# A new order of all steps, and single steps on another engine, in a gated linear attention with a mixing layer behind it

## The chip, the cores and the metric

The kernel runs on one core of a Trainium2 chip, in one launch. The metric is the device time of that core in microseconds (us). The kernel before took 360.42 us as the median of three runs (359.86 to 361.05). The core has five engines that work side by side, each on its own instructions in the order in which the program holds them: TensorE (PE in the profile; its weight loads are PEld), VectorE (DVE), ScalarE (ACT), GpSimd (POOL) and SyncE (SP), which here only issues the transfers.

## The reference

The inputs are q, k, v and gate logits of shape (4, 8, 768, 48), four weights and nothing else. First a gated linear attention runs over the 768 tokens, then its output goes through a mixing layer:

```python
f = 1.0 / (1.0 + np.exp(-f_logit))
for t in range(S):
    state = f[:, :, t, :, None] * state + np.einsum('bhd,bhe->bhde', k[:, :, t], v[:, :, t])
    y[:, :, t] = np.einsum('bhd,bhde->bhe', q[:, :, t], state)
...
theta = x @ w_theta
zr, zi = x * np.cos(theta), x * np.sin(theta)
y = np.einsum('ts,bsd->btd', w_tok_r, zr) + np.einsum('ts,bsd->btd', w_tok_i, zi)
u = x + y
return u + np.maximum(u @ w_ch, 0.0)
```

Here x is the attention's output with the 8 heads side by side (4, 768, 384). The weights come as float64, so that the kernel reads them as pairs of 32-bit words and decodes them to float32 itself. If some gate's product underflows, a second, slow program in the same kernel computes everything anew; it does not run on these inputs.

## The kernel before

The work is cut into 24 chunks of 128 tokens, six per batch. What is done for a chunk, and later for a group of three chunks (384 output tokens), is cut into named steps, each a small function. The table `ORDER` (line 53) lists 1169 step names; the loop at line 570 calls each step's function in that order, with a counter per name, so that the third `sc` is the scores of chunk 2. Since all five engines are scheduled by hand, the order of a step's instructions on its engine is its place in the table. A letter behind a slash says on which engine a step runs that could run on several: `/D` DVE, `/A` ACT, `/P` POOL; without one it is the usual engine of its function. Semaphores are set from the data: an instruction waits for what it reads and for the buffer that it writes, and for nothing else.

The steps that the prediction speaks of:

- `lf lq lk lv lw` load gates, q, k, v and a piece of a weight (SP).
- `gc go gs ge` turn the gate logits into running products: a clamp (line 237), two activations, a scan on DVE (247) and two activations (254, 255). `gp` copies the last column (POOL, 258).
- `gq` and `gk` multiply q (262) and k (267) by these products.
- `ke` transposes the keys (PE, 309), `kt` copies them out of PSUM; `sc` is the scores (298), `ma` their mask (304); `up` the state's update (323), `sa` and `st` add it (331, 335), `sm` fades the state (339); `qs` and `ou` are the output (354, 362), `xc` copies it, `xt` turns it (372), `xs` keeps it.
- `d1 d2 d3` decode a weight (183 and 193, 194 on DVE, 188 on ACT); `d4` and `d5` split it into a rounded part and a rest (218), since batches 1 to 3 use three products of rounded parts where batch 0 multiplies float32 as it is.
- `xh xl` split x (394), `th` is x @ w_theta (403), `tn se ab tr` reduce the angle and take sine and cosine, `ro` rotates x (436), `zh zl` split the result (443).
- `f0 f1 f2` are the token-mixing products (459), 48 of each; `v` adds them to x (463), `uh ul` split u (470), `c` is the channel product (477), `cv` the last addition (491), `so` the store (495).

What is on PE is therefore the same 4320 matmuls in any order. Tiles lie in pools with a fixed number of buffers: three each for f, q and k, one for the gates' products p, six for the rotated x and the weights' raw words, four banks of PSUM for the products.

Of the kernel before, what the change touches and what calls it, by code (L numbers as in the profile page):

```python
# [17 lines left out]
B, H, S, D = 4, 8, 768, 48  # L18
DM = H * D
P = 128  # L20
# [30 lines left out]


ORDER = (
# [36 lines left out]
)  # L90


# [608 lines left out]
```

## Time and profile before

| | before |
|---|---|
| median of three runs | 360.42 us |
| the profiled execution | 358.93 us |
| its span, from the first to the last instruction | 357.2 us |
| PE busy | 323.4 us (91%) |
| PEld busy | 284.8 us (80%) |
| DVE busy | 273.1 us (76%) |
| ACT busy | 186.6 us (52%) |
| POOL busy | 142.8 us (40%) |
| bytes moved | 45.55 MB |
| mean granted clock of TensorE | 0.980 of its 2.4 GHz |

The profile shows one execution. Busy time is the time in which an engine executes at least one instruction; the mean beside a group is that of one instruction from its start to its end, and instructions of one engine overlap a little, so the sum of a group's lengths is more than its busy time. An engine that waits for a semaphore is idle, but an instruction that has begun and is held up inside the engine counts as busy and shows as a longer one.

### The profile page before, as it was taken

The page shows a single profiled execution, that of the slowest core. Times are in us where ns is not written, and L with a number is a line of the kernel's source. Part 1 is how long each engine was busy: PE and PEld are TensorE (multiplying, and loading weights), DVE is VectorE, ACT ScalarE, POOL GpSimd, SP SyncE. Part 2 cuts the span into 40 slices and gives each one's busy share as a digit, 9 for nine tenths or more (in the row PEclk, how much of TensorE's full clock was granted, in tenths as well). Part 3 has the DMA queues.
Part 4 walks back from the last instruction along what each step waited for, and adds up shares of the span by engine and source line. Part 5 has one row for each costly group of instructions (what it writes and reads, how often), then busy time and mean ns, then how long its engine had stood idle before and what let it go on. Part 6 is the DMA issues. An engine that isn't in the chain of part 4 may idle for free.

```text
span 357.2 us, 10034 instructions
## 1 busy us (share of the span) xinstructions
PE 323.4 (91%) x4320; PEld 284.8 (80%) x4320; DVE 273.1 (76%) x402; ACT 186.6 (52%) x302; POOL 142.8 (40%) x122
## 2 busy tenths in 40 slices
PE   0689998799997699989999999999999999999992
PEld 0577675657754597978999999999999989999991
DVE  3999999999999989995889588996582766720331
ACT  5778988665856474846387252893224525200000
POOL 4426408660707705996588206604020512111000
PEclk9999999899999699999999999999999999999997
DMA  7888996158563225424040243503030200000112
GB/s 252 299 278 294 349 344 225 52 199 268 194 229 120 80 63 176 148 83 171 1 165 29 68 135 127 179 2 134 0 122 2 97 3 2 22 2 22 42 43 80
DMA packets 21651, 45.55 MB, mean 128 GB/s; under 512 B 2400, under 2 KB 5472, under 8 KB 21600
## 3 DMA queue, kind: packets, MB, share of 16 engines
q1 hardware_dynamic: 21600, 44.84, 37.0%
q8 instruction: 36, 0.59, 0.7%
q14 instruction: 15, 0.12, 0.1%
HBM read 40.11 MB, written 4.72 MB: 126 GB/s over the span
## 4 chain that ended last, share of the span: by engine, by line
PE 42%; DVE 5%; ACT 2%; DMA 1%; issue 1%; DVEq 0%; ACTq 0%
PE pm L459 23%; PE pch L477 8%; PE pth L403 4%; PE py L362 2%; DVE f L247 1%; PE sk L298 1%; PE pxt L372 1%; PE py L354 1%; PE sk L323 1%; PE psk L309 1%; DVE xl L394 1%; DVE k L267 1%; DMA out_dram<-ut 1%; DVE uhl L144 1%; DVE ut L491 0%
## 5 line engine op out<-in xcount | busy, mean ns | idle before, releaser
L459 PE MATMUL pm<-wp,z 128*128 128x384 f32 x648 | 119.2, 337 | 0.8 <-DVE ut L144 0.4
L459 PEld LDWEIGHTS pm<-wp,z 128*128 128x128 f32 x648 | 112.2, 188 | 2.0 <-DVE ut L144 0.8
L459 PE MATMUL pm<-value,z 128*128 128x384 f32 x144 | 49.9, 493 | 0.7 <-DVE value L194 0.7
L262 POOL TENSOR_TENSOR q<-q,p 128x512 f32<-128x512 f32 x20 | 31.1, 1553 | 39.0 <-ACT p L254 11.8
L459 PEld LDWEIGHTS pm<-value,z 128*128 128x128 f32 x144 | 27.1, 195 | 17.2 <-DVE value L194 1.4
L477 PE MATMUL pch<-uhl,wch 128*128 128x384 f32 x216 | 40.4, 339 | 0.0
L470 POOL TENSOR_TENSOR uhl<-ut,uhl 128x384 fp32r<-128x384 f32 x16 | 18.8, 1178 | 47.4 <-ACT uhl L144 35.0
L477 PEld LDWEIGHTS pch<-uhl,wch 128*128 128x128 f32 x216 | 37.4, 188 | 0.3
L247 DVE TENSOR_TENSOR_SCAN f<-carry,f 128x512 f32<-128x512 f32 x24 | 31.6, 1319 | 2.2 <-ACT f L243 2.2
L443 POOL TENSOR_TENSOR z<-w,z 128x768 fp32r<-128x768 f32 x12 | 23.6, 1970 | 21.8 <-ACT z L144 11.4
L309 PE MATMUL psk<-ident,k 128*128 128x128 f32 x96 | 16.9, 304 | 16.8 <-DVE k L267 16.5
L267 DVE SCALAR_TENSOR_TENSOR k<-f,k 128x512 f32<-128x512 f32 x24 | 27.6, 1150 | 2.8 <-ACT f L255 2.7
L491 DVE SCALAR_TENSOR_TENSOR ut<-pch,ut 128x384 f32<-128x384 f32 x24 | 13.0, 550 | 21.0 <-PE pch L477 20.9
L309 PEld LDWEIGHTS psk<-ident,k 128*128 128x128 f32 x96 | 12.0, 153 | 21.0 <-POOL q L262 9.3
L144 ACT CAST uhl<-ut 128x384 fp32r<-128x384 f32 x14 | 7.0, 508 | 41.1 <-PE pch L477 33.9
L436 DVE TENSOR_TENSOR w<-w,x 128x768 f32<-128x768 f32 x18 | 21.5, 1197 | 7.8 <-ACT w L427 7.8
L237 POOL TENSOR_SCALAR f<-f 128x512 f32<-128x512 f32 x11 | 18.0, 1636 | 17.4 <-DMA v<-in_v_dram 10.8
L463 DVE TENSOR_TENSOR ut<-pm,ut 128x384 f32<-128x384 f32 x24 | 13.1, 548 | 14.6 <-PE pm L459 14.6
L403 PE MATMUL pth<-wth,xh 128*128 128x384 f32 x108 | 23.0, 347 | 0.1
L254 ACT ACTIVATE p<-f 128x512 f32<-128x512 f32 x24 | 15.2, 632 | 12.6 <-DVE f L247 7.0
L298 PE MATMUL sk<-q,k 48*64 48x64 f32 x768 | 18.2, 233 | 3.8 <-DVE st L335 3.4
L323 PE MATMUL sk<-v,ktok 64*64 64x48 f32 x704 | 18.3, 235 | 3.4 <-DVE ktok L144 1.8
(84 smaller groups left out, 624.5 us busy)
## 6 DMA issues: line engine op xcount, KB each, us to landing
v<-in_v_dram SPq DMA_DIRECT2D x24, 384.0 KB, 4.4
f<-in_f_dram SPq DMA_DIRECT2D x24, 256.0 KB, 3.3
q<-in_q_dram SPq DMA_DIRECT2D x24, 256.0 KB, 4.1
k<-in_k_dram SPq DMA_DIRECT2D x24, 256.0 KB, 4.5
raw<-in_w_r_dram SPq DMA_DIRECT2D x12, 384.0 KB, 4.8
raw<-in_w_i_dram SPq DMA_DIRECT2D x12, 384.0 KB, 5.3
out_dram<-ut SPq DMA_DIRECT2D x24, 192.0 KB, 2.0
raw<-in_w_theta_dram SPq DMA_DIRECT2D x3, 384.0 KB, 6.0
```

The lines of the kernel that those rows point to most:

```text
L247: nc.vector.tensor_tensor_scan(fl, carry[:, pairs(h)].rearrange("p n t -> p (n t)"), fl, 0.0, ALU.mult, ALU.add)
L262: on(nc.vector).tensor_tensor(qt, qt, ps_[m][:, pairs(h)], op=ALU.mult)
L267: nc.vector.scalar_tensor_tensor(kt, loaded["f", m][:, pairs(h)], E_TOP, kt, op0=ALU.min, op1=ALU.mult)
L298: nc.tensor.matmul(out[HALF[j ^ t], j, p, :], kt[r, p, HALF[t]], qt[r, p, HALF[t]], start=True, stop=True)
L309: nc.tensor.transpose(psks[m][:, p, :], loaded["k", m][:, p, :], ident)
L323: nc.tensor.matmul(out[HALF[j], t, p, :], kts[m][HALF[t], p, HALF[j]], vs[m][HALF[t], 0, h * D:(h + 1) * D], start=True, stop=True)
L403: nc.tensor.matmul(pths[m], l, r, start=(n == 0), stop=(n == len(ms) - 1))
L436: nc.vector.tensor_tensor(zs[m] if full else w, w, xs[m].unsqueeze(1).to_broadcast([P, 2, DM]), op=ALU.mult)
L443: on(nc.vector).tensor_tensor(zs[m][:, 0], ws[m], zs[m][:, 1], op=ALU.subtract)
L459: nc.tensor.matmul(pms[g, d], l, r, start=(s == 0 and i == 0), stop=(s == NC - 1 and i == len(ms) - 1))
L470: on(nc.vector).tensor_tensor(us[g, d][:, 0], uts[g][:, d, :], us[g, d][:, 1], op=ALU.subtract)
L477: nc.tensor.matmul(pcs[g, d], l, r, start=(es[0] == 0 and n == 0), stop=(es[-1] == KD - 1 and n == len(ms) - 1))
```

## The change

Only the table `ORDER` differs. It has the same 1169 steps, all in a new order, and some have another engine behind the slash. The first and the last line of it:

```diff
-    "lf gc go lf lf gs ge lq lk gk gc/P gc go go gs lv lw lq ke kt gs up gp lk d1 gq/P sc sa ge gk ke lf st lk qs",
+    "lf lf gc go gc go lw gs lq lk lk gs d1 lq ge gp d2 gk ke gq d3 lf gc/P lv lf sc ge gk kt up sa st lw gq/P go",
...
-    "uh/D ul c c rv so cv cv cv so cv",
+    "c c c cv cv ul f1 f1 v uh ul/P f2 v uh/D ul c c c rv cv cv cv cv so so so so",
```

How many steps of a kind stand on which engine, where this differs:

| step | before | after |
|---|---|---|
| `gq` | 4 DVE, 20 POOL | 7 DVE, 17 POOL |
| `sm` | 6 DVE, 14 POOL | 10 DVE, 10 POOL |
| `ul` | 8 DVE, 16 POOL | 13 DVE, 11 POOL |
| `zl` | 6 DVE, 12 POOL | 12 DVE, 6 POOL |
| `d5` | 4 DVE, 10 POOL | 7 DVE, 7 POOL |
| `xl` | 12 DVE, 6 POOL | 10 DVE, 8 POOL |
| `kt` | 17 ACT, 7 DVE | 20 ACT, 4 DVE |
| `tn` | 9 ACT, 15 DVE | 14 ACT, 10 DVE |
| `xc` | 17 ACT, 7 DVE | 21 ACT, 3 DVE |
| `xs` | 15 ACT, 9 DVE | 11 ACT, 13 DVE |
| `xh` | 11 ACT, 7 DVE | 10 ACT, 8 DVE |
| `uh` | 14 ACT, 10 DVE | 13 ACT, 11 DVE |
| `zh` | 9 ACT, 9 DVE | 10 ACT, 8 DVE |
| `d4` | 9 ACT, 5 DVE | 10 ACT, 4 DVE |
| `ab` | 13 ACT, 11 DVE | 14 ACT, 10 DVE |

No wait and no semaphore is added; the changed file has one line less, so its line numbers behind the table are one lower.

The program's start on DVE, before (the number behind a name is the chunk or the weight piece, the one behind the underscore only tells tiles apart; k0 is the key product of chunk 0, raw0 the first weight's words):

```order
L237 TENSOR_SCALAR f0_92<-f0_92 128x512
L247 SCALAR_TENSOR_TENSOR f0_92<-carry_67,f0_92 128x512
L267 SCALAR_TENSOR_TENSOR k0_108<-f0_92,k0_108 128x512
L237 TENSOR_SCALAR f2_100<-f2_100 128x512
L247 SCALAR_TENSOR_TENSOR f1_98<-carry_67,f1_98 128x512
L247 SCALAR_TENSOR_TENSOR f2_100<-carry_67,f2_100 128x512
L183 TENSOR_SCALAR raw0_120<-raw0_120 128x768
```

And in the changed order, at the same place:

```order
L236 TENSOR_SCALAR f0_92<-f0_92 128x512
L236 TENSOR_SCALAR f1_94<-f1_94 128x512
L246 SCALAR_TENSOR_TENSOR f0_92<-carry_67,f0_92 128x512
L246 SCALAR_TENSOR_TENSOR f1_94<-carry_67,f1_94 128x512
L182 TENSOR_SCALAR raw0_103<-raw0_103 128x768
L266 SCALAR_TENSOR_TENSOR k0_109<-f0_92,k0_109 128x512
L261 TENSOR_TENSOR q0_107<-q0_107,p0_118 128x512
```

The first key product has moved behind the scan of chunk 1 and the first instruction of the first decoding, and the first q product has come to DVE.

POOL between the gate copies of chunks 12 and 14, before (q is the q product, st the fade, uhl the split of u, xl that of x, wp that of a weight, z that of the rotated x):

```order
L258 COPY pes_83<-p12_1512 128x4
L262 TENSOR_TENSOR q13_1598<-q13_1598,p13_1754 128x512
L339 TENSOR_TENSOR st12_1780<-st12_1780,pes_83 128x192
L470 TENSOR_TENSOR uhl11_1776<-ut1_703,uhl11_1776 128x384
L258 COPY pes_83<-p13_1754 128x4
L394 TENSOR_TENSOR xl9_1888<-ut3_1795,xh9_1797 128x384
L470 TENSOR_TENSOR uhl12_1793<-ut1_703,uhl12_1793 128x384
L262 TENSOR_TENSOR q14_1788<-q14_1788,p14_1905 128x512
L258 COPY pes_83<-p14_1905 128x4
```

And in the changed order:

```order
L257 COPY pes_83<-p12_1485 128x4
L338 TENSOR_TENSOR st10_1510<-st10_1510,pes_83 128x192
L442 TENSOR_TENSOR z7_1592<-w7_1335,z7_1592 128x768
L217 TENSOR_TENSOR wp02_1691<-value2_362,wp12_1198 128x768
L257 COPY pes_83<-p13_1694 128x4
L257 COPY pes_83<-p14_1784 128x4
```

Two q products, two splits of u and one of x have left this stretch, and a split of z and one of a weight have come.

DVE before the key product of chunk 17, before (sa, st and sc rows belong to `sa`, `st` and `ma`, ut to `v` or `cv` or `xs`, w to `se`):

```order
L331 TENSOR_TENSOR mid16_2417<-sk15_2384,st15_2355 128x192
L463 TENSOR_TENSOR ut2_1084<-pm21_1799,ut2_1084 128x384
L144 COPY ut4_2237<-pxt13_2442 128x3x128
L247 SCALAR_TENSOR_TENSOR f17_2096<-carry_67,f17_2096 128x512
L335 TENSOR_TENSOR st16_2461<-sk15_2384,mid16_2417 128x192
L463 TENSOR_TENSOR ut2_1084<-pm22_2253,ut2_1084 128x384
L304 TENSOR_TENSOR sc15_2486<-sk15_2384,causal_75 128x512
L267 SCALAR_TENSOR_TENSOR k17_2342<-f17_2096,k17_2342 128x512
```

And in the changed order:

```order
L413 SCALAR_TENSOR_TENSOR w12_2270<-w12_2270,pth12_2260 128x384
L469 TENSOR_TENSOR uhl22_2320<-ut2_1098,uhl22_2320 128x384
L330 TENSOR_TENSOR mid15_2365<-sk14_2297,st14_2199 128x192
L143 COPY ut4_2129<-pxt13_2367 128x3x128
L303 TENSOR_TENSOR sc14_2372<-sk14_2297,causal_75 128x512
L334 TENSOR_TENSOR st15_2384<-sk14_2297,mid15_2365 128x192
L490 SCALAR_TENSOR_TENSOR ut2_1098<-pch20_2374,ut2_1098 128x384
L143 COPY ktok16_2392<-psk16_2387 128x512
L266 SCALAR_TENSOR_TENSOR k17_2363<-f17_2169,k17_2363 128x512
```

In the changed order the key product of chunk 17 stands behind the scores of chunk 14, before it stood behind those of chunk 15; its scan has moved ahead of this piece.

## Rows read from the trace of the kernel before

**Rows 1.** Busy time by stretches. A row gives the stretch and its length in us, then the busy time of PE, PEld, DVE, ACT and POOL with the number of their instructions, the granted clock, the share of DMA and GB/s.

```profile
0.00:156.78 156.78, 131.70 (x2099) 98.94 (x2099) 147.23 (x202) 110.51 (x177) 79.12 (x73) 0.97 0.60 204
156.78:164.19 7.41, 6.88 (x38) 5.98 (x38) 6.02 (x11) 2.72 (x4) 6.05 (x5) 1.00 0.57 179
156.78:350.04 193.26, 191.74 (x2221) 185.90 (x2221) 125.25 (x200) 76.05 (x125) 63.68 (x50) 1.00 0.21 67
350.04:357.17 7.13, 0.00 (x0) 0.00 (x0) 0.58 (x2) 0.00 (x0) 0.00 (x0) 0.69 0.27 91
```

**Rows 2.** The longest entry for PE of the view of waits: engine, tile and line, what it waited for, us in total, how often, the longest.

```profile
PE psk L309 <- DVE k L267: 16.5, 6, 9.3
```

**Rows 3.** Pieces of the timelines of POOL, PE and DVE: start, length, engine, line and what it writes and reads; in brackets the idle time before it and what ended that.

```profile
7.35 1.27 POOL L262 TENSOR_TENSOR q<-q,p 128x512 f32<-128x512 f32 x1
...
100.53 7.26 PE L459 MATMUL pm<-value,z 128*128 128x384 f32 x22
...
153.70 2.53 POOL L218 TENSOR_TENSOR wp<-value,wp 128x768 fp32r<-128x768 f32 x1
...
154.48 2.30 DVE L267 SCALAR_TENSOR_TENSOR k<-f,k 128x512 f32<-128x512 f32 x1
...
156.83 0.66 PE L309 MATMUL psk<-ident,k 128*128 128x128 f32 x4 [0.97 <-DVE k L267]
...
191.57 0.60 PE L309 MATMUL psk<-ident,k 128*128 128x128 f32 x4
```

**Rows 4.** Pieces of DVE's timeline in which no POOL instruction reaches far into an instruction.

```profile
13.80 0.68 DVE L267 SCALAR_TENSOR_TENSOR k<-f,k 128x512 f32<-128x512 f32 x1
...
41.53 0.53 DVE L183 TENSOR_SCALAR raw<-raw 128x768 int32<-128x768 int32 x1
...
42.45 0.94 DVE L436 TENSOR_TENSOR z<-w,x 128x768 f32<-128x768 f32 x1
...
44.33 0.34 DVE L331 TENSOR_TENSOR mid<-sk,st 128x192 f32<-128x192 f32 x1
44.60 0.67 DVE L304 TENSOR_TENSOR sc<-sk,causal 128x512 f32<-128x512 f32 x1
45.20 1.21 DVE L247 TENSOR_TENSOR_SCAN f<-carry,f 128x512 f32<-128x512 f32 x1
46.33 0.93 DVE L193 SCALAR_TENSOR_TENSOR raw<-raw 128x768 int32<-128x768 int32 x1
47.29 0.96 DVE L194 SCALAR_TENSOR_TENSOR value<-raw 128x768 int32<-128x768 int32 x1
```

**Rows 5.** The same kinds as groups over the whole kernel: count, then busy time in us and the mean of one in ns, then idle time before them.

```profile
L267 DVE SCALAR_TENSOR_TENSOR k<-f,k 128x512 f32<-128x512 f32 x24 | 27.6, 1150 | 2.8 <-ACT f L255 2.7
L436 DVE TENSOR_TENSOR w<-w,x 128x768 f32<-128x768 f32 x18 | 21.5, 1197 | 7.8 <-ACT w L427 7.8
L304 DVE TENSOR_TENSOR sc<-sk,causal 128x512 f32<-128x512 f32 x24 | 16.3, 679 | 1.7 <-PE sk L298 1.7
L194 DVE SCALAR_TENSOR_TENSOR value<-raw 128x768 int32<-128x768 int32 x13 | 16.2, 1249 | 0.4
L193 DVE SCALAR_TENSOR_TENSOR raw<-raw 128x768 int32<-128x768 int32 x14 | 15.9, 1139 | 0.0
```

**Rows 6.** Pieces of PE in the chain that ended last: start, length, what, number of matmuls.

```profile
240.50 0.44 PE psk L309 x4
...
257.65 0.65 PE py L362 x32
258.29 0.47 PE sk L298 x31
...
260.28 1.04 PE pm L459 x6
261.32 1.56 PE pth L403 x9
...
263.93 0.33 PE pxt L372 x3
```

**Rows 7.** Groups of the moved steps, on DVE and on POOL, columns as in rows 5.

```profile
L262 POOL TENSOR_TENSOR q<-q,p 128x512 f32<-128x512 f32 x20 | 31.1, 1553 | 39.0 <-ACT p L254 11.8 <-DMA q<-in_q_dram 9.7 <-PE py L362 8.8
L443 POOL TENSOR_TENSOR z<-w,z 128x768 fp32r<-128x768 f32 x12 | 23.6, 1970 | 21.8 <-ACT z L144 11.4 <-DVE z L144 7.2 <-ACT w L419 3.2
L470 POOL TENSOR_TENSOR uhl<-ut,uhl 128x384 fp32r<-128x384 f32 x16 | 18.8, 1178 | 47.4 <-ACT uhl L144 35.0 <-DVE uhl L144 12.3
L218 POOL TENSOR_TENSOR wp<-value,wp 128x768 fp32r<-128x768 f32 x8 | 17.0, 2126 | 0.2
L339 POOL TENSOR_TENSOR st<-st,pes 128x192 f32<-128x192 f32 x14 | 12.0, 857 | 20.6 <-DVE st L335 19.5 <-PE pth L403 1.0
L394 POOL TENSOR_TENSOR xl<-ut,xh 128x384 fp32r<-128x384 f32 x6 | 9.2, 1532 | 14.3 <-DVE w L436 13.5 <-DVE xh L144 0.8
L443 DVE TENSOR_TENSOR z<-w,z 128x768 fp32r<-128x768 f32 x6 | 6.1, 1010 | 0.1
```

**Rows 8.** The timeline at the program's start: SP's first three transfers and the first key product.

```profile
0.80 1.34 SPq L516 DMA_DIRECT2D f<-in_f_dram  x3
...
7.83 1.33 DVE L267 SCALAR_TENSOR_TENSOR k<-f,k 128x512 f32<-128x512 f32 x1 [1.36 <-ACT f L255]
```

**Rows 9.** A line of the page's part 6: what is loaded, how often, KB each, median us from issue to landing.

```profile
raw<-in_w_theta_dram SPq DMA_DIRECT2D x3, 384.0 KB, 6.0
```

68 rows, old and new, of the table ORDER are left out of this document.

## The prediction

> **What bounds the kernel now.** I read the kernel's time by stretches first [rows 1], then the longest waits of TensorE (PE) [rows 2], then single instructions of VectorE (DVE), which is the engine that the waits name.
>
> The stretches [rows 1] show two stages. Up to 156.78 us DVE is busy for 147.23 us and PE for 131.70. From 156.78 to 350.04 us PE is busy for 191.74 of 193.26 us and DVE for 125.25. So DVE sets the pace first and PE afterwards; then 7.13 us follow the last matmul, in which the last results are stored. The border is a release that the trace shows: the transposes of the sixteenth chunk's keys (`ke` number 15, counted from 0) start at 156.83 us after a wait for DVE's key product of line 267 [rows 3]; six such waits make 16.5 us [rows 2].
>
> The second thing to see is that many DVE instructions are far longer than their own work. That key product takes 2.30 us at 154.48, beside a GpSimd (POOL) instruction that runs from 153.70 to 156.23 [rows 3]; undisturbed it takes 0.68 us [rows 4]. Over the kernel its mean is 1150 ns, the rotation's (line 436) 1197 where 0.94 us is its own, the decoding's (193, 194) 1139 and 1249 where 0.93 and 0.96 are. The mask of line 304, which reads PSUM, has a mean of 679 ns, and an undisturbed one takes 0.67 us [rows 4, 5]. So an SBUF instruction of DVE that falls under a POOL instruction waits for it, and a PSUM one does not.
>
> **The change part by part.** All engines issue in program order, so the order decides what stands ahead of what. I add up, for a given step, the own work that stands ahead of it on PE and on DVE.
>
> Prices on PE: a product step of batches 1 to 3 is six matmuls, 1.04 us; a channel or angle step of nine is 1.56; the small ones are 0.65 (`ou`), 0.47 (`sc`, `qs`, `up`), 0.44 (`ke`) and 0.33 (`xt`) [rows 6]. A product step of batch 0 is four matmuls out of a run of 22 that took 7.26 us [rows 3], 1.29 when the last one's pipelined end is taken off, and an angle step of batch 0 is six, 1.94. All steps together: 36 x 1.29 + 108 x 1.04 + 6 x 1.94 + 18 x 1.56 + 24 x 1.56 + 66 for the small ones = 302 us. The order doesn't change this sum. PE ends at 350, so 48 us are lost on it before its end.
>
> Prices on DVE: the undisturbed rows [rows 4], and for a kind without a row there the length of one of the same shape; 0.055 us is taken off per step, because a row runs on by about that much past the start of the next.
>
> Before, at `ke` 15: PE has 115.3 us ahead of it, DVE 123.7 us up to the key product (16 scans 19.4, 16 decodings of three instructions 39.2, 16 key products 10.9, 10 rotations 9.5, 13 masks 8.8, 26 state steps 9.1, 68 smaller ones 36.8, less 181 x 0.055). DVE is idle for 156.78 - 147.23 = 9.6 us [rows 1]. What is left of 156.8 is disturbance: 156.8 - 123.7 - 9.6 = 23.5 us. POOL's own work ahead of it is 57.5 us (14 q products at the 1.27 of [rows 3], and at the shortest lengths of their kinds 7 clamps, 15 copies, 9 fades, 4 weight splits, 5 x splits, 6 u splits and 2 z splits), so DVE loses 0.41 us per microsecond of POOL's own work. PE is then 156.8 - 115.3 = 41.5 us behind, and of the 48 it loses in all, 6.5 come later.
>
> The change moves work between engines. POOL gives up 3 q products, 4 state fades, 5 splits of u, 6 splits of z and 3 of the weights and gets 2 splits of x; with the means of [rows 7] that is 4.7 + 3.4 + 5.9 + 11.8 + 6.4 - 3.1 = 29 of its 142.8 us. DVE gets these for 3 x 0.68 + 4 x 0.36 + 5 x 0.55 + 6 x 0.96 + 3 x 0.95 - 2 x 0.56 = 13.7 us, and hands 5.4 us net to ScalarE (ACT): 3 key copies, 5 roundings, 4 x copies and 3 small steps leave it, 4 copies of the turned x and 2 casts come. So +8.3 us for DVE. ACT gets about 4 us more and has one table load fewer; with 110.5 of 156.78 us busy [rows 1] it hides that, and if that cover were gone it would cost these 4.
>
> The order decides where this falls. At `ke` 14 the changed order has 109.9 us on PE and 119.0 on DVE; before, these were 110.9 and 118.7. So the two are level there, but POOL's work ahead is 37.2 instead of 52.8 us: 4 q products, 5 splits of u and 3 of x fewer are the bulk of it. At 0.41 that is 15.3 us of disturbance: 119.0 + 9.6 + 15.3 = 143.9, and PE is 34.0 behind. After that the changed order keeps DVE loaded for longer: at `ke` 17 it has 147.2 us ahead on DVE and 142.2 on PE (before 142.0 and 148.3, PE well ahead in work and DVE no longer deciding), with 49.1 on POOL. I add 2 us of DVE idle time for these 28 us, as it is idle for 7.41 - 6.02 = 1.4 in the first 7 behind the border before [rows 1]: 147.2 + 11.6 + 20.1 = 178.9, and PE is 36.7 behind. At `ke` 20 it is 176.7 + 11.6 + 27.8 - 181.7 = 34.4. The largest decides: 36.7 against 41.5.
>
> For what comes later, `ke` 17 started at 191.57 before [rows 3], 43.3 behind, so 48 - 43.3 = about 5 us came after it. I take the same 5: DVE stays close behind PE up to `ke` 20, so I give no credit there. PE then ends at 302 + 36.7 + 5 = 343.7. The tail has the same last stores and the flag's branch: 7.1. The span is 350.8 us.
>
> The start is one small term. DVE's first decoding now stands ahead of the first key product, and its two transfers of w_theta are issued third and fourth. In the trace the fourth transfer is issued at about 0.80 + 1.34 = 2.1 us [rows 8], and one of w_theta lands 6.0 us after its issue [rows 9]: 8.1 + 0.53 + 0.68 = 9.3, where the key product ended at 7.83 + 1.33 = 9.16 [rows 8]. That is 0.2 us, which I leave inside the idle time above.
>
> The sum is made against the profiled execution: its span of 357.2 and its time of 358.93, 1.7 more. So 352.5 is the forecast in its terms. The median of the runs shown is 360.42, 1.5 above; carried over, 354.0 us.
>
> **The rivals.**
>
> Separation works. If the new order really keeps the two engines' SBUF work apart in time, the rate of 0.41 falls. Nothing in a semaphore enforces this: the orders only say what follows what, and a POOL instruction still starts when its inputs are there. In the list the next DVE step behind a POOL step is an SBUF one in 40 of 70 cases, against 41 of 89 before, which speaks against it. For it speaks that the moved steps are those that met DVE. With 0.15, about a third, as the short copies and whatever the order doesn't hold apart still meet, the largest lag is `ke` 13: 112.5 + 9.6 + 0.15 x 35.2 - 101.0 = 26.4, the end 302 + 26.4 + 5 + 7.1 + 1.7 = 342.2, or 344 carried over.
>
> It turns out slower: DVE stays the bound through the second batch. The mechanism is the place between `ke` 14 and `ke` 17, where the changed order puts 28.2 us of DVE work against 32.3 on PE, with DVE 9 us behind already. If the disturbance follows DVE's own SBUF work, not POOL's (23.5 / 123.7 = 0.19 per us, and the SBUF share of DVE's work rises as the POOL steps come to it), then at `ke` 17 it is 28.0: 147.2 + 11.6 + 28.0 - 142.2 = 44.6, and with 5 later, up to 8 if the closeness at `ke` 20 costs PE again, the time is 302 + 44.6 + 5 to 8 + 8.8 = 360.4 to 363.4, or 362 to 365 carried over. It decides from a disturbance of 26.5 us at `ke` 17, where the lag passes 43. The Trainium skill ("Perfetto Trace Analysis", Optimizing Scalar/DVE Operations) warns that offloading between GpSimd and VectorE might not help because they share an SBUF read port; by that rule the 20% of POOL's work taken off would bring nothing and this rival would be the likely one. What the trace shows in [rows 3] is DVE waiting for the rest of one POOL instruction, 156.23 - 154.48 = 1.75 us and then its own 0.68, near the 2.30 measured; that ties the loss to POOL's time, so I give this rival the smaller chance.
>
> No change: the gain at the border is real, but PE gives it back in waits spread over `ke` 17 to 23, where PE has only 3 to 24 us more work ahead of it than DVE, and had 14 to 34 before from `ke` 18 on. That asks for 7 us more than the 5 taken: about 360.
>
> **How the numbers follow.** The forecast gets 0.41, separation 0.27, no change 0.11, slower 0.21. Predicted: 354.0 us. The bounds of the disturbance rate, 0.15 and the 0.19 by DVE's work, give 344 to 363, and this range leaves out the end of the slower case. A measurement of this kernel tells no change from a difference of about 0.3%, some 1.1 us. So faster has 0.41 + 0.27 = 0.68, the same 0.11, slower 0.21.
>
> **What would show it.** In the changed profile: DVE's busy time before PE runs without holes should fall by some 8 us for the same work; the mean of line 267's instruction (266 there) below 1150 ns; POOL's busy time near 114 us; the last wait of PE for DVE's key product near `ke` 17 at about 179 us, with PE busy from there to about 344. The prediction is wrong if means of the SBUF forms stay as they are and DVE is over 19.5 of 20 us busy beyond 190, or if a long wait on PE names a transfer or ACT.

## The result, and the profile after

The changed kernel takes 343.48 us (median of four runs, 342.64 to 346.18); the kernel before took 360.74 us on the same chip (median of four). The ratio is 0.9535, with a 95% interval of 0.9477 to 0.9594: faster, and just below the low end of the predicted range (344). The profiled execution took 343.03 us with a span of 341.0.

The stretches first. The rows are of the kernel before, with the columns of [rows 1]: three stretches in which PE's clock can be compared, and, as the last, all that lies ahead of the end of chunk 17's key product.

```profile
0.00:60.00 60.00, 46.30 (x955) 34.73 (x956) 53.63 (x83) 48.51 (x81) 26.61 (x34) 1.00 0.85 293
60.00:115.00 55.00, 49.22 (x564) 32.66 (x562) 53.83 (x67) 36.83 (x58) 25.28 (x20) 0.97 0.52 180
115.00:157.00 42.00, 36.36 (x584) 31.72 (x585) 39.99 (x54) 25.18 (x39) 27.45 (x21) 0.92 0.32 105
...
0.00:187.01 187.01, 161.32 (x2501) 127.22 (x2502) 169.76 (x236) 128.17 (x206) 100.78 (x87) 0.97 0.56 191
```

The same view of the changed kernel, and below it the stretches that answer to the later two of [rows 1]:

```profile
0.00:60.00 60.00, 47.04 (x950) 34.80 (x951) 50.09 (x83) 48.79 (x82) 27.11 (x33) 1.00 0.82 279
60.00:115.00 55.00, 52.95 (x569) 35.01 (x570) 50.88 (x77) 39.42 (x63) 15.28 (x15) 1.00 0.56 196
115.00:157.00 42.00, 41.85 (x669) 38.87 (x662) 36.58 (x60) 30.64 (x50) 16.85 (x12) 1.00 0.44 136
0.00:171.44 171.44, 156.29 (x2459) 122.59 (x2462) 151.60 (x242) 127.30 (x209) 65.91 (x66) 1.00 0.59 198
172.06:334.70 162.64, 162.64 (x1834) 159.33 (x1828) 101.17 (x169) 59.99 (x101) 44.21 (x37) 1.00 0.20 66
334.70:341.00 6.30, 0.32 (x2) 0.00 (x0) 0.93 (x2) 0.00 (x0) 0.00 (x0) 0.91 0.30 101
```

To 60 us there is little to choose. From 60 to 157 us PE is busy for 94.8 of 97 us, where before it was busy for 85.6, and POOL's busy time there falls from 52.7 to 32.1 us. From 115 us on PE is the bound, 42 us earlier than before. The granted clock, 0.97 and 0.92 before, is 1.00. Up to the end of chunk 17's key product, at 187.01 us before and 171.44 after, DVE's busy time falls from 169.76 to 151.60 us, by 18 us where the prediction had named some 8; its idle time there is 17.3 us before and 19.8 after.

The waits of PE, which answer to [rows 2]: six for the key product, 16.5 us in all, have become two, of which one is the start. The start was 9.3 us before and is 10.4 now, so behind it 7.2 us have become 0.2.

```profile
PE psk L308 <- DVE k L266: 10.6, 2, 10.4
PE py L361 <- DVE sc L303: 2.0, 2, 1.1
PE pm L458 <- DVE value L193: 0.6, 2, 0.4
```

The groups that answer to [rows 5]. The form that reads PSUM (the mask) is as long as before; the SBUF forms have come down towards their own time (0.68, 0.94, 0.93 and 0.96 us in [rows 4]).

```profile
L266 DVE SCALAR_TENSOR_TENSOR k<-f,k 128x512 f32<-128x512 f32 x24 | 19.3, 807 | 2.0 <-ACT f L254 1.2 <-DMA k<-in_k_dram 0.8
L435 DVE TENSOR_TENSOR w<-w,x 128x768 f32<-128x768 f32 x18 | 17.7, 985 | 4.6 <-ACT w L426 4.6
L303 DVE TENSOR_TENSOR sc<-sk,causal 128x512 f32<-128x512 f32 x24 | 16.3, 681 | 3.3 <-PE sk L322 3.1 <-PE sk L297 0.2
L192 DVE SCALAR_TENSOR_TENSOR raw<-raw 128x768 int32<-128x768 int32 x14 | 13.3, 951 | 0.1
...
L193 DVE SCALAR_TENSOR_TENSOR value<-raw 128x768 int32<-128x768 int32 x13 | 13.0, 1002 | 0.4
```

The page has POOL at 110.1 us (142.8 before) and DVE at 254.1 (273.1).

Where the 16.2 us of span went, in the prediction's own terms: PE is 172.06 - 142.2 = 29.9 us behind at `ke` 17 instead of 43.3, so 13.4 come from there; behind that it loses 335.0 - 302 - 29.9 = 3.1 instead of 4.7; and the tail is 6.0 instead of 7.1. (The last product runs 0.32 us into the last row above, to 335.02.)

One measure is used for all runs below. The **excess** is the sum, over DVE's instructions that read no PSUM and start ahead of PE's transposes of `ke` 17, of their length less the shortest one of the same kind and shape in the two traces. Before, 148 instructions have 36.1 us of it; after, 157 have 11.0. Sorted by who was there first: where a POOL instruction was already running when the DVE instruction began, 71 instructions lost 34.8 us before and 44 lost 9.1 after; where POOL began while DVE's was running, 20 and 21 lost 0.4 and 0.3; the rest, 57 and 92, met no POOL instruction and lost 0.9 and 1.5. And of POOL's busy time up to there (105.0 and 65.9 us) DVE spent 74% in SBUF instructions before and 56% after, while outside POOL's time the share rose from 69 to 76%. So the separation is there, in the times at which things run.

### The profile page after: what moved, and what is told of

Same layout as the page of the kernel before. It is cut to its first block, busy times and chain, and to the rows that moved or that the text cites. A ratio compares the mean times of both kernels' runs of the same rounds, so it can differ in the third digit from the quotient of the medians.

```text
span 341.0 us, 10019 instructions
## 1 busy us (share of the span) xinstructions
PE 319.9 (94%) x4320; PEld 282.5 (83%) x4320; DVE 254.1 (74%) x412; ACT 187.9 (55%) x309; POOL 110.1 (32%) x103
## 4 chain that ended last, share of the span: by engine, by line
PE 73%; DVE 11%; DMA 8%; ACT 2%; issue 2%; SPq 1%; POOL 1%; DVEq 0%; POOLq 0%
PE pm L458 37%; PE pch L476 11%; PE pth L402 9%; PE py L361 4%; DMA raw<-in_w_i_dram 3%; PE sk L297 3%; PE psk L308 3%; PE sk L322 3%; PE pxt L371 3%; PE py L353 2%; DVE raw L192 2%; DMA k<-in_k_dram 2%; DMA v<-in_v_dram 2%; DMA q<-in_q_dram 1%; DVE value L193 1%
## 5 line engine op out<-in xcount | busy, mean ns | idle before, releaser
L458 PEld LDWEIGHTS pm<-wp,z 128*128 128x128 f32 x648 | 112.6, 188 | 0.3
L458 PEld LDWEIGHTS pm<-value,z 128*128 128x128 f32 x144 | 26.4, 190 | 17.2 <-DVE value L193 1.8
L469 POOL TENSOR_TENSOR uhl<-ut,uhl 128x384 fp32r<-128x384 f32 x11 | 13.3, 1213 | 65.3 <-ACT uhl L143 63.5
L246 DVE TENSOR_TENSOR_SCAN f<-carry,f 128x512 f32<-128x512 f32 x24 | 29.7, 1246 | 0.7 <-ACT f L242 0.7
L261 POOL TENSOR_TENSOR q<-q,p 128x512 f32<-128x512 f32 x17 | 25.7, 1510 | 8.9 <-DMA q<-in_q_dram 6.7
L143 ACT COPY x<-py 128x384 f32<-128x384 f32 x21 | 10.0, 479 | 32.8 <-PE py L361 25.6
L257 POOL COPY pes<-p 128x4 f32<-128x4 f32 x24 | 10.0, 418 | 55.2 <-ACT p L253 55.1
L308 PEld LDWEIGHTS psk<-ident,k 128*128 128x128 f32 x96 | 12.2, 153 | 13.6 <-issue 11.2
L236 POOL TENSOR_SCALAR f<-f 128x512 f32<-128x512 f32 x11 | 19.4, 1764 | 12.0 <-DMA f<-in_f_dram 12.0
L393 POOL TENSOR_TENSOR xl<-ut,xh 128x384 fp32r<-128x384 f32 x8 | 8.7, 1092 | 41.7 <-DVE xh L143 22.5
L361 PEld LDWEIGHTS py<-v,sc 64*64 64x64 f32 x768 | 15.0, 140 | 8.2 <-DVE sc L303 4.0
L253 ACT ACTIVATE p<-f 128x512 f32<-128x512 f32 x24 | 15.2, 631 | 11.6 <-POOL q L261 5.5
L435 DVE TENSOR_TENSOR w<-w,x 128x768 f32<-128x768 f32 x18 | 17.7, 985 | 4.6 <-ACT w L426 4.6
```

Of the source, the lines that this page charges most:

```text
L143: (nc.scalar.copy if on(usual) is nc.scalar else on(usual).tensor_copy)(dst, src)
L236: on(nc.vector).tensor_scalar(ft, ft, F_MIN, None, op0=ALU.max)
L246: nc.vector.tensor_tensor_scan(fl, carry[:, pairs(h)].rearrange("p n t -> p (n t)"), fl, 0.0, ALU.mult, ALU.add)
L253: nc.scalar.activation(ps_[m][:, pairs(h)], ft, AF.Exp, scale=-1.0)
L261: on(nc.vector).tensor_tensor(qt, qt, ps_[m][:, pairs(h)], op=ALU.mult)
L308: nc.tensor.transpose(psks[m][:, p, :], loaded["k", m][:, p, :], ident)
```

## The experiments

All runs, with the ratio to the kernel before on the same chip; `ke` 17 is the start of PE's transposes, excess and POOL's busy time (with some 1.2 us at the program's start that belong to no step) are up to there.

| run | us | ratio, 95% | `ke` 17 at | excess | POOL busy |
|---|---|---|---|---|---|
| before | 360.74 | | 191.6 | 36.1 | 105.0 |
| changed | 343.48 | 0.948 to 0.959 | 172.1 | 11.0 | 65.9 |
| e1 order alone | 387.25 | 1.071 to 1.081 | 201.0 | 26.9 | 92.3 |
| e2 engines alone | 377.88 | 1.045 to 1.056 | 193.7 | 23.3 | 72.7 |
| e3 no steps on POOL | 363.28 | 1.006 to 1.014 | 187.2 | 3.1 | 10.1 |
| e4 extra work on POOL | 350.05 | 0.966 to 0.976 | 180.1 | 15.8 | 99.1 |
| e5 exchanged under POOL | 348.28 | 0.965 to 0.971 | 176.5 | 16.1 | 67.9 |
| e6 exchanged elsewhere | 343.37 | 0.950 to 0.958 | 172.4 | 11.0 | 65.8 |
| e7 new, then old | 347.81 | 0.961 to 0.968 | 173.8 | 12.2 | 68.4 |
| e8 start | 342.87 | 0.949 to 0.954 | 171.5 | 11.4 | 64.8 |
| e9 old, parted | 360.82 | 0.998 to 1.003 | 193.5 | 36.7 | 104.2 |
| e10 old, exchanged elsewhere | 361.70 | 1.003 to 1.007 | 193.1 | 35.8 | 103.7 |
| e11 start, and parted | 341.75 | 0.947 to 0.952 | 169.9 | 9.4 | 64.7 |
| e12 new order and POOL, old ACT | 375.34 | 1.035 to 1.048 | 194.9 | 17.2 | 65.6 |
| e13 new order and ACT, old POOL | 366.00 | 1.009 to 1.026 | 188.9 | 23.9 | 93.4 |

**Is it POOL that lengthens DVE's instructions?** Every `/P` is taken out of the table (e3):

```diff
-gq d3 lf gc/P lv lf sc ge gk kt up sa st lw gq/P go
+gq d3 lf gc lv lf sc ge gk kt up sa st lw gq go
```

> The changed kernel, with all 70 steps that it has on POOL put on DVE (only the 24 copies of gates' last columns stay). If POOL is what lengthens DVE's instructions, all SBUF forms take their own time (key product 0.68 us, rotation 0.95), and DVE has 277.8 us of own work instead of 239.1: at ke 13 126.7 + 12 - 101.0 = 38 us behind, at ke 17 167.1 + 15 - 142.2 = 40, against 29.8: about 353 (350 to 356). If the lengthening comes from something else (transfers, ACT), the means stay at the changed kernel's (key product 0.81, scan 1.25) and DVE needs 11 us more: above 360.

The means of the groups in e3:

```profile
L245 DVE TENSOR_TENSOR_SCAN f<-carry,f 128x512 f32<-128x512 f32 x24 | 29.1, 1217 | 1.5 <-ACT f L241 1.5
...
L434 DVE TENSOR_TENSOR w<-w,x 128x768 f32<-128x768 f32 x18 | 17.1, 949 | 4.1 <-ACT w L425 4.1
...
L265 DVE SCALAR_TENSOR_TENSOR k<-f,k 128x512 f32<-128x512 f32 x24 | 16.3, 682 | 2.2 <-ACT f L253 1.5 <-DMA k<-in_k_dram 0.7
```

They are the undisturbed lengths, with the same transfers and the same steps on ACT: POOL is the cause. The time is 10 us above what I expected. Up to `ke` 17 DVE has 20 us more of own work, as expected, but is idle for 24.3 us where I had put 15.

**What does work on POOL cost that the order has no place for?** In e4, 57 idle products stand behind every second POOL step:

```diff
+    fn["xx"] = lambda n: [nc.gpsimd.tensor_tensor(idle, carry[:, i, :], carry[:, i, :], op=ALU.mult) for i in range(3)]
-gc/P lv lf sc ge gk kt up sa st lw gq/P go
+gc/P lv lf sc ge gk kt up sa st lw gq/P xx go
```

> The changed kernel with idle work added on POOL: behind every second of its steps up to ke 17, three products of 128x128 from a constant tile to a spare one, which nothing waits for (57 instructions, some 0.37 us each, 21 us). Theory O in its strong form (the DVE instructions stand where POOL's don't matter, so any POOL work is kept apart): 0.09 x 21 = 2 us more on DVE, time 343 to 346. If POOL work that the order has no place for meets DVE at the old rate: 0.41 x 21 = 8.6 us more, PE 38 us behind: 350 to 353. Between the two lies what PE's slack takes up.

350.05 us, with `ke` 17 8 us later, as the second theory has it; but only 4.8 of these are excess, 0.14 us for each of the 33 us by which POOL is busier up to there, and 3.3 are more idle time of DVE (180.1 - 156.7 against 172.1 - 152.0). The added products took 0.64 us each where I had put 0.37, so that the second theory's time came out by luck. So the excess per microsecond of POOL's busy time is no constant of the kernel: it is 0.34 before, 0.17 after and 0.16 here.

**Order or engines?** e1 has the new order with each step on its old engine, e2 the old order with the new engines:

```diff
# e1, the new order
-gq d3 lf gc/P lv lf sc ge gk kt up sa st lw gq/P go
+gq/P d3 lf gc lv lf sc ge gk kt up sa st lw gq/P go
# e2, the old order
-gk gc/P gc go go gs lv lw lq ke kt gs up gp lk d1 gq/P sc
+gk gc gc/P go go gs lv lw lq ke kt gs up gp lk d1 gq sc
```

> The new order, with the old engine for every step (POOL has its 115 us of own work again, not 90). Theory O, the order itself keeps the SBUF work of DVE and POOL apart: DVE loses about 0.09 us per us of POOL's own work, as in the changed kernel (4.4 us over 49.1 at ke 17); at ke 17 that is 141.7 us of own work + 19.8 idle + 0.09 x 70.0 = 167.8, not later than in the changed kernel, so the time stays near its 343.5 (342 to 347) and the key product's mean stays near its 0.81 us. Theory A, what counts is which steps are on POOL: the rate is back at 0.35 to 0.41, DVE is through at 141.7 + 11.6 + 24.5 to 28.7 = 178 to 182 and PE is 36 to 40 us behind instead of 29.8: 349 to 354, key product's mean near 1.1 us.

> The old order, with the new engine for every step but one (rounding of x number 5 stays on ACT). Theory A, the assignment is what counts: the rate is about 0.09, at ke 15 DVE is through at 126.6 + 9.6 + 0.09 x 42.8 = 140.1, PE 25 us behind, and the time comes near the changed kernel's (343 to 348). Theory O, the order: the rate stays at 0.41, 126.6 + 9.6 + 17.5 = 153.7 at ke 15, PE 38.4 behind instead of 41.5: 355 to 359, means of the SBUF forms near those of before (key product 1.0 to 1.15 us).

Both theories fail, in the same way: each half alone makes the kernel slower than before, by 27 and 18 us, and both together make it 17 us faster. The excess falls with either half, to 26.9 and 23.3 us, but 65 and 73% of POOL's time still lies beside SBUF work, more than there is outside POOL's time (61 and 66%): no separation. And the excess is only a part of the loss. Up to `ke` 17 e1 is 29 us later than the changed kernel; 16 us are excess, and DVE is idle for 37.5 us instead of 19.8. The longest waits of PE in e1:

```profile
PE psk L309 <- DVE k L267: 12.6, 4, 10.7
PE pm L459 <- DVE z L436: 4.1, 1, 4.1
PE pch L477 <- POOL uhl L470: 4.0, 3, 2.8
PE pth L403 <- DVE ut L463: 3.2, 2, 1.9
PE pch L477 <- DVE ut L491: 2.8, 1, 2.8
PE sk L323 <- DVE ktok L144: 2.4, 1, 2.4
PE pxt L372 <- DVE x L144: 2.1, 1, 2.1
```

Behind the start (10.7 us) no single wait is large; many readers come a little late. A step on another engine than its place was made for is late there, and everything that its engine issues behind it waits with it; that is how I read these rows.

e12 and e13 split this: the new order with either only POOL's list as changed, or only the exchanges between ACT and DVE.

```diff
# e12
-ma ou xs sa st d4 gc lf d2 d3 d1 kt xc gp lv lv gq/P gc/P ge
+ma ou xs sa st d4/D gc lf d2 d3 d1 kt xc/D gp lv lv gq/P gc/P ge
# e13
-gq d3 lf gc/P lv lf sc ge gk kt up sa st lw gq/P go
+gq/P d3 lf gc lv lf sc ge gk kt up sa st lw gq/P go
```

> The new order with the new POOL steps, and only the exchanges between ACT and DVE taken back (77 steps on their old engine). DVE has 152.2 us of own work ahead at ke 17 instead of 147.2. Theory P, the order fits POOL's list, and that is what the run with all old engines broke: the excess up to ke 17 stays near 11 us (under 15), PE is some 35 us behind, 347 to 351. Theory E, each step's place fits its engine, whichever it is: the steps now on the wrong one of ACT and DVE come late for their readers as those of POOL do, 360 or more.

> The counterpart: the new order, ACT and DVE share their steps as in the changed kernel, and POOL has its old steps (75 steps on their old engine; DVE has 136.7 us ahead at ke 17 instead of 147.2, POOL 70.0 instead of 49.1). Theory P: nearly all of the loss of the run with all old engines comes back, 375 to 390, excess 22 to 27 us up to ke 17. Theory E: about half of it, 360 to 368.

By the time, theory E holds in both: with 75 steps wrong on POOL 366.0, with 77 wrong between ACT and DVE 375.3. The excess of e12, 17.2 us, is above theory P's 15 too; the exchanges that I had booked as 5.4 us of relief for DVE and four us on ACT cost 32 us when they are taken back. The first and the last of these waits of PE in e12 show how: copies of x, which the changed kernel has on ACT, are issued by DVE behind its other work, and PE waits for them.

```profile
PE pxt L371 <- DVE x L143: 3.6, 1, 3.6
PE pm L458 <- DVE z L435: 3.1, 1, 3.1
...
PE py L353 <- DVE x L143: 1.2, 1, 1.2
```

**Does the gain rest on what stands beside POOL?** e5 and e6 each exchange ten pairs of neighbours on DVE in the changed kernel, a PSUM reader and an SBUF instruction; in e5 where POOL ran, in e6 where it didn't. Two of the ten each (the list around them is left out):

```diff
# e5
-ma ou xc sc tn gs
+gs ma ou xc sc tn
-se d3 th
+d3 se th
# e6
-sa gs ge st d3 gp
+gs sa ge d3 st gp
```

> The changed kernel with ten pairs of neighbours on DVE exchanged between 47 and 144 us, where in its trace an instruction that reads PSUM ran under a POOL instruction and an SBUF one came right behind it: now the SBUF one comes first and meets POOL. What was left of the POOL instruction at these places is 7.3 us in all. Theory F, the gain rests on this fit in time: DVE loses most of that, 5 to 7 us more than the 11.0 that it loses up to ke 17, PE waits for part of it, 346 to 350. Theory R, the fit is an average over many instructions and DVE has room (19.8 us idle up to ke 17): excess up by under 3 us and the time within 1.5 of 343.5.

> The counterpart: ten such pairs between 58 and 160 us exchanged at places where no POOL instruction ran, and the SBUF instructions are as long or longer (12 us instead of 10). Theory F: nothing meets that didn't, excess up by under 2 us, and the time stays within 2 of 343.5, under that of the other exchange by 2 or more. Theory W, what counts is only that each step comes at its place for its readers: each exchange delays a PSUM reader alike, so this one costs as much as the other or more.

The excess rises by 5.1 us in e5 and by nothing in e6, and the time by 4.8 us and by nothing. Theory F holds. One of the ten, first in the timeline of the changed kernel, where the addition of line 490 lies under POOL's instruction and the rounding of u (line 143) behind it takes 0.83 us:

```profile
121.51 1.82 POOL L217 TENSOR_TENSOR wp<-value,wp 128x768 fp32r<-128x768 f32 x1
...
122.25 0.56 DVE L490 SCALAR_TENSOR_TENSOR ut<-pch,ut 128x384 f32<-128x384 f32 x1 [0.64 <-PE pch L476]
122.72 0.83 DVE L143 CAST uhl<-ut 128x384 fp32r<-128x384 f32 x1
```

and in e5, where POOL's instruction begins 0.04 us ahead of the rounding, which then waits it out:

```profile
124.10 1.83 POOL L217 TENSOR_TENSOR wp<-value,wp 128x768 fp32r<-128x768 f32 x1
124.14 2.00 DVE L143 CAST uhl<-ut 128x384 fp32r<-128x384 f32 x1
126.06 0.55 DVE L490 SCALAR_TENSOR_TENSOR ut<-pch,ut 128x384 f32<-128x384 f32 x1
```

**Can the kernel before be mended in the same way?** e9 parts nine pairs there that met, e10 exchanges nine that didn't.

```diff
# e9
-gk ke kt ma ou gp
+ma gk ke kt ou gp
# e10
-gp d1 d2 se gk
+gp se d1 d2 gk
```

> The kernel before, with every step on its engine, and only nine pairs of neighbours on DVE exchanged between 43 and 192 us: where in its trace an SBUF instruction lost time under a POOL instruction and the next one, which reads PSUM, had its data already, the PSUM one now comes first. The SBUF instructions lost 7.3 us at these places. Theory F, the time is lost by who stands beside POOL: the excess up to ke 17 falls from 36.1 us by 5 to 7, DVE sets the pace there, and three of the places lie ahead of PE's longest waits (63, 113 and 118 us) after which the clock fell: 350 to 355. Rival, moved instructions only meet the next POOL work: excess down by under 2 us, time 358 to 361.

> The counterpart on the kernel before: nine such exchanges between 42 and 138 us, a PSUM reader ahead of an SBUF instruction, where no POOL instruction ran. Theory F: nothing is won in excess (within 2 us of 36.1), and the time stays within 2 of 360. If it is the earlier PSUM reader that helps PE, and not POOL's neighbourhood, this one gains as much as the other.

Theory F fails here. The excess stays at 36.7 us and the time at 360.8. Summed over the SBUF steps that start ahead of `ke` 17 before, those that got shorter gave 8.3 us and others took 8.9. In [rows 3] the key product at 154.48 us took 2.30; in e9 it takes 0.68 at 156.46, but the scan ahead of it now begins 0.03 us behind a POOL instruction:

```profile
151.18 1.85 POOL L443 TENSOR_TENSOR z<-w,z 128x768 fp32r<-128x768 f32 x1
151.21 2.90 DVE L247 TENSOR_TENSOR_SCAN f<-carry,f 128x512 f32<-128x512 f32 x1
152.98 2.74 POOL L218 TENSOR_TENSOR wp<-value,wp 128x768 fp32r<-128x768 f32 x1
154.03 2.50 DVE L436 TENSOR_TENSOR w<-w,x 128x768 f32<-128x768 f32 x1
...
156.46 0.68 DVE L267 SCALAR_TENSOR_TENSOR k<-f,k 128x512 f32<-128x512 f32 x1
```

e10 came out as theory F has it for that run: the excess stays at 35.8 us, and the time, 361.70, is 0.5% above before.

Where POOL has the next instruction ready, a DVE instruction that escapes one meets the next. POOL is busy for 105.0 of 191.6 us there (0.55), and for 65.9 of 172.1 (0.38) after. That this share alone decides whether parting works is not shown, and two runs speak against it: e2 has a share of 0.38 and an excess of 0.32 us per microsecond of POOL's busy time, e4, with short instructions added, a share of 0.55 and 0.16. By these two what counts is where POOL's instructions lie against DVE's.

**Where in the program is the gain made?** e7 runs the changed table up to `ke` 17 and all other steps behind it as before.

```diff
# behind "ke" number 17
-the rest of the new table
+the steps that are left, in the old table's order, on their old engines
```

> The changed order and engines up to and with ke 17, and behind it all remaining steps in the old order on their old engines. If the gain is made up to ke 17 (PE 29.8 us behind there instead of 43.3) and the old rest costs what it did (48.4 - 43.3 = 5.1 us more, instead of 2.9), the time is 346 to 348. If the later part of the order is needed as well (its steps meet again, PE waits for splits that come late), it is above 351.

347.81, with `ke` 17 at 173.8 us: the gain is made up to there, and the later part, with the seam, is worth some 4 us.

**The start, and a version that beats both.** e8 moves the first steps of the changed table, e11 also parts five pairs.

```diff
# e8 and e11
-lf lf gc go gc go lw gs lq lk lk gs d1 lq ge gp d2 gk ke gq d3
+lf lf lk gc go gc go lw gs lq lk gs lq ge gp gk ke d1 d2 gq d3
# e11
-lw ab f1 ma ou
+lw ma ab f1 ou
```

> The changed kernel with only its first steps moved: the first keys are loaded ahead of w_theta, and the first decoding comes behind the first key product. In the changed kernel that product waited for its keys until 9.52 us, while the activation that it needs was through at 8.02; it can start at about 8.1, PE at 8.9 instead of 10.35. If PE keeps this lead to the end, 342.0; if the next waits (PE 17.1 us behind at ke 2, 19.4 at ke 3) are set by DVE's own work and by loads, the lead is lost and the time stays 343.5.

> The changed kernel with the first steps moved as in the run on the start, and five pairs parted by the rule of the run on the kernel before: 3.3 us of DVE's loss at 43, 61, 94, 101 and 143 us. PE still waits 3.6 us in all for DVE between 20 and 113 us, and not at all behind that, so of the 3.3 us some 1 to 2 can reach the end: 341 to 342.5 against 342.9; if DVE no longer sets PE's pace there, no change.

In e8 PE begins at 8.55 us instead of 10.35, and 0.5 us of the lead are left at `ke` 17 (171.5 against 172.1). 342.87 against 343.48 lies within both intervals, so e8 alone is inconclusive. e11 takes another 2.0 us of excess away and comes to 341.75; its interval (0.9472 to 0.9517) ends below the changed kernel's ratio of 0.9535, though the two intervals overlap. Its median is the lowest here; that it beats the changed kernel is likely, not certain.

## Why the prediction was wrong, point by point

**The direction and the place were right.** PE loses its time up to `ke` 17 and hardly any behind it; e7 confirms it. PE's own 302 us and DVE's own 147.2 at `ke` 17 stand. Less than 1150 ns for line 266's instruction (807) and near 114 us for POOL (110.1) came as named; the wait at `ke` 17 didn't come.

**The step that failed is the rate of 0.41 us of disturbance per microsecond of POOL's work, kept for the changed kernel.** At `ke` 17 I had 147.2 + 11.6 + 20.1 = 178.9. The trace has the key product's end at 171.44 with DVE busy for 151.60, so 19.8 us idle, and 171.4 - 147.2 - 19.8 = 4.4 of disturbance: 0.09 per us of POOL's own 49.1. The term was too large by 15.7 us; DVE's idle time, which I had built on the 9.6 us ahead of `ke` 15 and which was too small by 8.2, hid half of that, and PE came out 29.9 behind instead of 36.7. (By the same working e3, with nothing to disturb it, comes to -4.7, so the prices of DVE's steps are some 3% high and the true disturbance is larger; the excess of 11.0 does not depend on them.) With the early disturbance gone, `ke` 17 decides nothing: PE's last wait of over 0.15 us ends at 113 us.

**Why the rate fell.** I had treated it as a property of the engines and the order as something that only moves work about. It depends on which instruction begins while POOL is running, as the count by who came first shows, and as e5 against e6 shows by a test. Less work on POOL alone doesn't lower it: e2, with nearly as little of it as the changed kernel, has 0.32 us of excess per microsecond of POOL's busy time against 0.17. The Trainium skill ("SBUF — State Buffer", Who interferes with whom) states the rule: VectorE and GpSimd share a port pair that one instruction holds to its end, whoever starts first, and the other blocks; a VectorE instruction with one SBUF input outside the two-port modes takes no part. The trace agrees with who comes first: 0.4 us lost in 20 cases where DVE was first, 34.8 in 71 where POOL was; the rounding of 0.36 us that takes 2.00 beside a POOL instruction of 1.83; the mask, one of whose inputs is in PSUM, at 679 and 681 ns. POOL pays in its turn: over the whole kernel before, 50 of its TENSOR_TENSOR instructions began while an SBUF instruction of DVE was running, and were 20.8 us longer in all than the shortest of their kinds; the other 28 lost 0.4 (after, 11.8 in 33 and 0.4 in 26).

**The argument against "separation works" was unsound.** I counted which DVE step follows a POOL step in the list, 40 of 70 against 41 of 89. But a POOL instruction starts when its data are there and POOL is free, not when its neighbour in the list does, so the list can't tell. The rival with 0.27 is what happened: 344 forecast, 343.5 measured. That it is so near is partly luck: its lag of PE, 26.4 us at `ke` 13, is 28.9 there in the trace and 29.9 at `ke` 17, and what it takes for later and for the tail (5 and 7.1 us) is 3.1 and 6.0.

**The separation of the change into terms was wrong too.** "Minus 29 us for POOL, plus 8.3 for DVE" and "the order" were added up. e1, e2, e12 and e13 show that they can't be: each part without the rest is 1.7 to 7.6% slower than before. A step's place is right only for the engine that runs it.

**The slower rival**, disturbance by DVE's own work, is refuted: DVE's own SBUF work up to `ke` 17 rose (by the shortest lengths, from 106.9 to 112.6 us) and the excess fell to a third. Beside it stood the Trainium skill's warning ("Perfetto Trace Analysis", Optimizing Scalar/DVE Operations) that offloading between VectorE and GpSimd might not help. In e3 taking all of POOL's steps back costs 20 us: DVE has 20 us more of own work up to `ke` 17 and only 8 less of excess. Its steps also stand in an order that was made for other engines, so this is no clean price of the offloading.

**The start** was mis-sized: +0.2 us forecast, 1.04 measured (PE's first transpose at 10.35 against 9.31). I followed the decoding; what is late is the transfer of the first keys, which the new list issues behind w_theta's:

```profile
1.72 0.90 SPq L169 DMA_DIRECT2D raw<-in_w_theta_dram  x2
...
3.14 0.91 SPq L515 DMA_DIRECT2D k<-in_k_dram  x2
...
7.39 0.63 ACT L254 ACTIVATE f<-f 128x512 f32<-128x512 f32 x1
...
9.52 0.69 DVE L266 SCALAR_TENSOR_TENSOR k<-f,k 128x512 f32<-128x512 f32 x1 [0.80 <-DMA k<-in_k_dram]
```

**What was missing** is the clock. Before, it was at the lower of its two levels (1.2 of 2.4 GHz) for a few microseconds behind PE's waits of 3.23 us (to 64.56) and 3.35 us (to 117.38). These are the two stretches, with the columns of [rows 1]:

```profile
66.05:69.46 3.41, 3.41 (x90) 2.99 (x80) 3.38 (x5) 3.38 (x6) 1.85 (x2) 0.50 0.02 5
117.25:124.07 6.82, 4.93 (x86) 4.32 (x87) 6.49 (x11) 3.50 (x6) 4.31 (x5) 0.50 0.07 25
```

Half of their length, 1.7 + 3.4 = 5 us of work at full speed, is the most that they cost; after, PE's longest wait behind the start is 1.1 us and the clock stays at 1.00 to PE's end. I had put this into the 41.5 us without naming it, so it came back as a gain that no term had. No run separates it from the waits themselves.

The rest: 5 us taken for what comes later were 3.1, the tail 6.0 for 7.1, ACT has two table loads fewer (22 for 24) and not one, and the profiled execution stands 0.5 us from the median, not 1.5.

## What to carry to other kernels

Where two engines block each other, don't carry a rate from one schedule to the next: find from the trace which instruction begins under a running one, and bound the new schedule by none of these meetings and by all. An order and an assignment of engines that were made together are one term; half of it can cost more than the whole brings. A local exchange took 2.0 us of excess away in e11 and none in e9, where the instruction that escaped met POOL's next one: look in the trace for what POOL runs at the new place.

## What the runs showed of the hardware that I had not expected

Whoever comes second pays, however close: 0.03 us behind POOL made a scan of 1.21 us last 2.90, and 0.04 us a rounding of 0.36 last 2.00; DVE instructions that began first lost 0.4 us in 20 cases together. The added POOL products of 128x128 (0.64 us in the mean) cost DVE 0.14 us per microsecond, against 0.34 for the mixture before, whose instructions are mostly of 1 to 2.7 us; no run tests whether their length is the reason.

Not every SBUF instruction of DVE waits for POOL, as the prediction had it. The rounding of x (`xh`) reads and writes SBUF and has the size of that of u, but takes 0.54 us where that one takes 0.36, alone and beside POOL. In e13 it begins with 1.75 us of a POOL instruction ahead of it and still takes 0.54; the split of a weight, 0.95 us by itself, waits there:

```profile
146.86 2.26 POOL L443 TENSOR_TENSOR z<-w,z 128x768 fp32r<-128x768 f32 x1
147.37 0.54 DVE L144 CAST xh<-ut 128x384 fp32r<-128x384 f32 x1
...
148.30 1.63 DVE L218 TENSOR_TENSOR wp<-value,wp 128x768 fp32r<-128x768 f32 x1
```
